# A new order of the whole instruction list, other engines for some copies and block sums, and 130 zero matmuls instead of 82

## The chip, the cores and the metric

The kernel runs on one core of a Trainium2 chip. The metric is the device time of one launch in microseconds (us), inputs in HBM at the start and the output in HBM at the end. Four compute engines work side by side, each on its own queue strictly in order: PE (matrix multiply, with its weight loads in the row PEld), DVE (vector), ACT (activation) and POOL (general purpose). SP only issues DMAs. An instruction that needs what another engine makes waits at the head of its queue, and everything behind it in that queue waits too.

## The reference

Cross attention in both directions between 512 tokens and 32 states for 8 batches and 8 heads, followed by a two layer network with a leaky activation.

```python
# x (8, 8, 512, 64), state (8, 8, 32, 64)
scores = scale * x @ state^T ; a  = softmax(scores)  ; xread = a  @ state
scores2 = scale * state @ x^T; a2 = softmax(scores2) ; sread = a2 @ x
attn = concatenate([xread, sread], axis=2)           # (8, 8, 544, 64)
x = attn.transpose(0, 2, 1, 3).reshape(8 * 544, 512)
h = x @ w_in                                          # w_in (512, 2048)
g = maximum(h, 0) + alpha * minimum(h, 0)
out = g @ w_out                                       # w_out (2048, 512), out (4352, 512)
```

## The kernel before

All tensors are held in 16 bit floats on chip; matmuls accumulate in 32 bit. The 512 tokens of a batch never pass through `xread`: since `xread @ w_in = a @ (state @ w_in)`, the kernel multiplies the states with `w_in` (step `m`, copied out of PSUM by `mo`) and then the softmax weights with that product (step `F`, or `f` for half a contraction, `h` in the profile). There are 16 column blocks of `h` for each of the batches 0 to 7. Each goes through two elementwise steps: `N` (ACT writes relu(-h), "neg") and `G` (DVE makes g from neg, 1 - alpha and h, into the tile "gp"). "Batch 8" is a ninth set of rows: the 256 state rows of all batches (`sread`), collected by `rd` and `rdo`, with its own `F.8`, `N.8`, `G.8` of half the width.

The second layer is done in two ways. Batch 0 uses plain matmuls (`S`, 2 of 128x512 each, copied out by `O`). Batches 1 to 8 use a seven product block scheme: `P.b.p.c` is a quarter of product p of batch b (4 matmuls of 128x256; 2 for batch 8), the sums and differences of blocks of g are made by `A.b.i.grp` ("s"), those of `w_out` by `T.i.part` ("ws"), and `Q` copies or adds the products out. The last output block of batch 7 is done by plain matmuls in three pieces (`M`, `MO`).

The softmax of the tokens' weights for batch b runs through four engines: `sc` (PE, scores), `sb` (DVE, 32x32 transposes), `smax` (DVE), `ssh` (POOL, subtract the maximum), `sexp` (ACT), `ssum` (DVE), `snorm` (POOL), `wb` (DVE, transposed back to "aT"). `F.b` needs `wb.b`. The other direction goes `tm` or `tx`, `ty` (maximum), `te` (ACT, exp), `tsum`, `tn` (normalise), `tt` (transposing DMA), `rd`. Batch 0 does the first chain in two halves, its steps having a third number 0 or 1.

Input loads that change the type are issued by POOL in its queue: `lx0`, `lx.b` (x), `lst` (states), `wi.f` and `wo.i` (quarters of the weights, 512 KB each as they land). x of batches 0 and 1 is transposed by PE (`xt`, copied by `xo`), of the others by a transposing DMA on SP's queue (`xd`). Half of x of batch 0 and the states of batch 0 come in by SP's and ACT's DMAs in 32 bits and are cast on chip (`xc`, `stc`); `stt` and `sto` are the transposition of batch 0's states and its copy, `str` and `sro` the same for all other states; `id` makes the identity matrix that the transposes need; `oma` makes 1 - alpha. `Z.k.n` issues n matmuls of zeros into PSUM bank k, whose result nobody reads.

The order of all of this is written out in the list `ORDER`, one word for each step; the loop at the end of the kernel issues the steps in that order, and each engine receives its own steps in the order of the list. In a word the numbers are the step's arguments; a last number is a PSUM bank (k0 to k5 are single banks; steps without one use a shared pair of banks called "two"), a last letter is the engine: a is ACT, v is DVE, p is POOL, and d (for `A`) an accumulating DMA issued by POOL. A bank is taken again only when the last reader of its former tile is done.

The list decides four things: the order on each queue, the bank of each PSUM tile, the engine of each copy and block sum, and how many zero matmuls stand where.

Of the kernel before, what the change touches and what calls it, by code (L numbers as in the profile page):

```python
# [29 lines left out]
smax.1 N.0.11 S.0.2.3 m.0.3 G.0.8 F.0.10.5 tn.0.1 T.0.0.p T.0.1.p S.0.0.3 mo.0.3.a.0 G.0.9 N.0.10  # L30
G.0.11 ssh.p.1 T.2.0.p S.0.3.0.3 mo.0.3.v.1 S.0.3.1 F.0.13.0 S.0.3.2 sexp.1 N.0.13 G.0.10 S.0.3.3
m.1.3 ssum.1 G.0.13 F.0.14.5 S.0.2.4 snorm.p.1 T.1.0.p N.0.14 G.0.14 S.0.1.4 wb.1 tt.0 F.0.12.0
N.0.12 G.0.12 S.0.0.4 F.0.15.5 S.0.3.4 mo.1.3.a.1 N.0.15 tsum.1 tn.1.0 S.0.1.5 G.0.15 S.0.0.5
# [2 lines left out]
F.1.0.2 O.0.0.a T.3.0.p G.1.3 S.0.1.7 N.1.0 S.0.3.5 smax.2 te.2.1 F.1.5.4 S.0.3.6 O.0.1.a G.1.0
F.1.1.5 N.1.5 ssh.p.2 S.0.3.7 G.1.9 N.1.1 F.1.2.1 O.0.3.a G.1.1 F.1.6.2 N.1.2 F.1.4.0 W.O.0.3 G.1.5
T.2.1.p F.1.8.3 sexp.2 W.O.0.2 P.1.1.0.5 G.1.2 N.1.4 rd.0.4 ssum.2 N.1.6 rd.1.1 rdo.0.a lx.4 P.1.1.1
rdo.1.a xd.3 F.1.11.4 G.1.4 N.1.8 snorm.p.2 F.1.12.1 te.2.0 G.1.6 F.1.10.0 N.1.11 G.1.8 m.2.3 N.1.10
F.1.15.2 G.1.11 F.1.13.3 N.1.12 A.1.3.0.p P.1.1.2 G.1.10 mo.2.3.a.1 W.O.0.1 P.1.2.0.4 mo.2.3.a.0  # L40
# [792 lines left out]
```

## Time and profile before

| | |
|---|---|
| median of 3 runs | 210.06 us (209.83 to 210.15) |
| span of the profiled execution | 208.5 us |
| median less that span (start and end of the launch that the span leaves out) | 1.6 us |
| PE busy in the span | 200.2 us, 96% |
| DVE, POOL, ACT busy | 175.2, 180.9, 145.5 us |

The profile covers one execution. The profiled execution's own launch time is not given apart from its span; the span and the 1.6 us around it make the median. The lines of the profile name the engine, the line of the kernel, the operation, what it writes and reads, and durations in us; "x16" is a count. Durations of matmuls include the time until the result lies in PSUM, so that those of neighbouring matmuls overlap: the spacing of starts, not the duration, is what a matmul costs in a stream. The step names used here are not in the profile; a step is found there by its line number (`N` is L551, `G` L569, `F` L519 and for batch 8 L528, `P` L668, `S` L588, `m` L486, `mo` L508, `Z` L245, `A` L645 and by DMA L621, `T` L616, `tn` L440 on ACT and L442 otherwise) and by its place in the list.

### The profile page before, as it was taken

What the parts mean: (1) busy time and instruction counts of PE and PEld (TensorE: products, weight loads), DVE (VectorE), ACT (ScalarE), POOL (GpSimd) and SP (SyncE); (2) the same over time, 40 slices, a digit from 0 to 9 for tenths busy, and PEclk for the clock granted to TensorE, in tenths of its full rate; (3) what the DMA queues carried; (4) which work ended last, traced back from release to release, by engine and by line L of the source; (5) the groups of instructions that cost most, each with busy time, mean ns of one, the idle gap of its engine ahead of it and who ended that gap; (6) DMA issues with size and microseconds to landing.
All of it is one profiled execution on the core that took longest, in us unless ns stands there. A gap on an engine that the chain in (4) does not pass through costs nothing.

```text
span 208.5 us, 5136 instructions
## 1 busy us (share of the span) xinstructions
PE 200.2 (96%) x2034; PEld 135.3 (65%) x2034; DVE 175.2 (84%) x273; ACT 145.5 (70%) x291; POOL 180.9 (87%) x119
## 2 busy tenths in 40 slices
PE   7789999999999999999999999999999999999993
PEld 6554344346557775766677776666678777888882
DVE  1697998999999999999999999998995987744431
ACT  4298996699998899988889579778654545451110
POOL 7579948999999999999999999979996972969960
PEclk9999999999999999999999999999999999999999
DMA  6999999599979949999997166035401144234143
GB/s 148 177 204 208 205 203 149 103 132 191 218 144 142 116 58 212 206 126 165 183 225 100 43 146 166 24 82 151 104 0 53 23 78 154 37 63 156 50 153 104
DMA packets 44793, 27.11 MB, mean 130 GB/s; under 512 B 22097, under 2 KB 42465, under 8 KB 44769
## 3 DMA queue, kind: packets, MB, share of 16 engines
q0 software_dynamic: 14192, 12.03, 38.5%
q1 hardware_dynamic: 29872, 14.23, 31.1%
q10 hardware_dynamic: 704, 0.52, 0.8%
q8 instruction: 16, 0.26, 0.5%
q14 instruction: 9, 0.07, 0.1%
HBM read 17.31 MB, written 8.91 MB: 126 GB/s over the span
## 4 chain that ended last, share of the span: by engine, by line
PE 70%; DVE 14%; ACT 5%; DMA 4%; POOL 3%; issue 2%; DVEq 0%; POOLq 0%
PE p L668 41%; PE h L519 18%; DVE gp L569 8%; DMA w_in_sb<-in_moe_w_in_dram 4%; PE h L528 3%; PE m_ps L486 3%; PE sr_ps L461 2%; ACT m L508 1%; DVE aT L397 1%; ACT neg L551 1%; DVE m L508 1%; POOL s L645 1%; ACT e L424 1%; POOL an L387 1%; PE o L588 1%
## 5 line engine op out<-in xcount | busy, mean ns | idle before, releaser
L551 ACT ACTIVATE neg<-h 128x512 f32<-128x512 f32 (+1 forms) x144 | 78.5, 583 | 27.4 <-PE h L519 18.5
L569 DVE SCALAR_TENSOR_TENSOR gp<-neg,oma_sb,h 128x512 f16<-128x512 f32 x128 | 89.0, 735 | 6.7 <-ACT neg L551 6.4
L519 PE MATMUL h<-aT,m 128*128 128x512 f16 x250 | 68.6, 379 | 0.3 <-DVE gp L569 0.3
L645 POOL TENSOR_TENSOR s<-gp,s 128x1024 f16<-128x1024 f16 x28 | 65.7, 2393 | 1.2 <-DVE gp L569 0.6
L668 PEld LDWEIGHTS <-gp 128*128 128x128 f16 x432 | 41.7, 98 | 13.9 <-issue 1.9
L668 PEld LDWEIGHTS <-s 128*128 128x128 f16 x368 | 35.2, 98 | 12.7 <-POOL s L645 1.7
L668 PE MATMUL p<-ws,s 128*128 128x256 f16 x248 | 37.3, 273 | 0.2 <-POOL s L645 0.2
L645 POOL TENSOR_TENSOR s<-gp 128x1024 f16<-128x1024 f16 x14 | 31.6, 2260 | 6.5 <-DVE gp L569 6.4
L519 PEld LDWEIGHTS <-m 128*128 128x128 f16 x250 | 23.6, 98 | 16.1 <-issue 3.3
L668 PE MATMUL p<-ws,gp 128*128 128x256 f16 x224 | 33.6, 273 | 0.0
L508 ACT CAST m<-m_ps 128x512 f16<-128x512 f32 x51 | 28.8, 600 | 4.8 <-PE m_ps L486 3.6
L668 PE MATMUL p<-w_out_sb,gp 128*128 128x256 f16 x208 | 30.6, 273 | 0.0
L371 POOL TENSOR_TENSOR ts<-ts,mx 128x1024 f32<-128x1024 f32 (+1 forms) x9 | 17.1, 1905 | 6.0 <-DVE mx L365 6.0
L668 PE MATMUL p<-w_out_sb,s 128*128 128x256 f16 x120 | 18.3, 273 | 0.0
L387 POOL TENSOR_TENSOR an<-ts,r 128x1024 f16<-128x1024 f32 (+1 forms) x9 | 16.3, 1808 | 1.8 <-DVE r L382 1.8
L588 PE MATMUL o<-w_out_sb,gp 128*128 128x512 f16 x64 | 16.6, 380 | 0.1
L621 POOL DMA_DIRECT2D gp<-gp x14 | 13.2, 962 | 3.4 <-issue 2.9
L569 DVE SCALAR_TENSOR_TENSOR gs<-neg,oma_sb,h 128x256 f16<-128x256 f32 x16 | 7.2, 478 | 8.2 <-ACT neg L551 8.2
L486 PE MATMUL m_ps<-w_in_sb,stT 64*32 64x512 f16 x256 | 11.7, 383 | 0.3 <-DMA w_in_sb<-in_moe_w_in_dram 0.2
L588 PEld LDWEIGHTS <-gp 128*128 128x128 f16 x64 | 5.9, 98 | 8.1 <-issue 1.3
L424 ACT ACTIVATE e<-sc,nb 128x512 f16<-128x512 f32 x16 | 11.0, 693 | 0.1
L699 ACT COPY p<-p 128x512 f32<-128x512 f32 x11 | 6.5, 588 | 6.4 <-PE p L668 6.4
(76 smaller groups left out, 248.9 us busy)
## 6 DMA issues: line engine op xcount, KB each, us to landing
out_dram<-c SPq DMA_DIRECT2D x27, 256.0 KB, 3.1
xg<-in_x_dram POOLq DMA_DIRECT2D x7, 512.0 KB, 8.7
gp<-gp POOLq DMA_DIRECT2D x14, 256.0 KB, 3.6
w_in_sb<-in_moe_w_in_dram POOLq DMA_DIRECT2D x4, 512.0 KB, 11.8
w_out_sb<-in_moe_w_out_dram POOLq DMA_DIRECT2D x4, 512.0 KB, 13.1
...
```

Of the source, the lines that this page charges most:

```text
L371: engine(e).tensor_tensor(ts, ts, over_blocks(cols(live["mx", b], j, S // N)), ALU.subtract)
L387: engine(e).tensor_tensor(blocks(cols(live["an", b], j, S)), blocks(cols(live["ts", b], j, S)), over_blocks(cols(live["r1", b], j, S // N) ...
L424: nc.scalar.activation(live["e2", b][:, g, :, :], live["sc", b][:, :, :, g, :].rearrange("p r j s -> p (r j) s"), EXP, bias=live["nb", b][ ...
L486: nc.tensor.matmul(t[N * k : N * (k + 1), :], st_head(b, h)[64 * r : 64 * r + 64, :], w_in_sb[64 * r : 64 * r + 64, c, 512 * f : 512 * (f ...
L508: copier(e)(m_tile(b)[:, f, g, :], live["mp", b, f][g])
L519: nc.tensor.matmul(h.rearrange("p (r j s) -> p r j s", r=2, j=2), ms[b][:, f, g, 128 * j : 128 * (j + 1)], weights(b, g), start=(g == 0), ...
L551: nc.scalar.activation(neg, h, RELU, bias=0.0, scale=-1.0)
L569: nc.vector.scalar_tensor_tensor(gt, negs.pop((b, jc)), oma_sb[:, jc : jc + 1], h, ALU.mult, ALU.add)
L588: nc.tensor.matmul(outs[b, q], token_cols(b, jc, q), w_out_sb[:, jc, :], start=(jc == 0), stop=(jc == n_jc - 1),)
L621: nc.gpsimd.dma_start(gp[:, 1, 0], gp[:, 1, 1], accum_op=ALU.add)
L645: engine(e).tensor_tensor(t, x, y, op)
L668: nc.tensor.matmul(chains[chain][:, t, :], lhs, rhs[:, i, :], start=(opens and i == 0 and t == 0), stop=(i == half_k - 1), skip_group_chec ...
```

## The change

The list `ORDER` is replaced from its first word to its last. In the new list

- there are 8 groups of zero matmuls (20, 16, 12, 18, 9, 24, 21, 10) instead of 10 (20, 9, 7, 6, 4, 3, 5, 12, 7, 9), all of them before the first `f` or `F` of batch 0 as before;
- 14 of the 50 block sums `A` made by POOL are given to DVE (10 of full size, 4 of batch 8), and 1 of the 8 `T`; the 14 made by a DMA stay;
- `tn`: POOL 2 instead of 6, ACT 9 instead of 10, DVE 5 instead of 0;
- copies `mo`: DVE 4 instead of 13, ACT 60 instead of 51; `Q`: DVE 27 instead of 31, ACT 28 instead of 24; `xo`: DVE 6, ACT 2 instead of 7 and 1; `rdo`: DVE 2, ACT 6 instead of 3 and 5; `sro`: one on DVE instead of both on ACT; `xc` has its two engines exchanged; `stc` is on ACT, for which the step takes an engine as an argument;
- all PSUM banks are given out anew.

The numbers of all other instructions and DMAs are the same. Only the parts of the two lists that are spoken of are shown.

```diff
 ORDER = """
-lx0 id lst stc xc.1.v xc.0.a oma wi.0 lx.1 Z.1.20 stt.0 Z.2.9 xt.0.1.0.1 xt.0.0.0.2 xo.0.1.0.v
-xo.0.0.0.v sto.a Z.0.7 sc.0.0 Z.0.6 xt.0.1.1.3 xt.0.0.1.4 str.0.5 sb.0.0 xo.0.0.1.v xo.0.1.1.a Z.1.4
-sc.0.1 smax.0.0 str.1.0 sro.0.a wi.1 sb.0.1 wo.0 smax.0.1 wi.2 ssh.p.0.0 sro.1.a sexp.0.0 Z.1.3 sc.0
-m.0.0.1.2 ssh.p.0.1 mo.0.0.a.0 Z.5.5 m.1.0.3.4 m.2.0.5.0 tm.0 mo.2.0.a.0 ssum.0.0 sexp.0.1
-mo.1.0.a.0 mo.2.0.a.1 wo.1 Z.1.12 m.3.0.1.5 Z.3.7 xt.1.1.0.3 snorm.p.0.0 mo.1.0.v.1 te.0.1
-mo.3.0.a.1 ssum.0.1 wb.0.0 xt.1.0.0.4 xo.1.1.0.v te.0.0 xo.1.0.0.v wi.3 xt.1.1.1.0 snorm.p.0.1 Z.3.9
-f.0.0.0.5 mo.0.0.a.1 xo.1.1.1.v xt.1.0.1.3 wo.2 f.0.2.0.4 tsum.0 m.1.1 wb.0.1 mo.3.0.a.0 xo.1.0.1.v
-m.0.1.0.2 mo.1.1.v.0 tn.0.0 mo.0.1.v.0 f.0.2.1 f.0.0.1 mo.1.1.a.1 mo.0.1.a.1 f.0.1.0.1 f.0.1.1
-F.0.3.3 m.4.0 N.0.0 N.0.1 F.0.5.2 N.0.2 F.0.4.0 G.0.0 G.0.1 N.0.3 G.0.2 F.0.7.5 N.0.5 N.0.4 G.0.3
-S.0.1.0.1 mo.4.0.a.0 S.0.0.0.4 mo.4.0.a.1 G.0.4 S.0.0.1 S.0.1.1 lx.2 N.0.7 m.0.2.3.0 sc.1 G.0.5
-mo.0.2.a.0 S.0.2.0.2 wo.3 G.0.7 m.1.2.5.3 mo.0.2.a.1 mo.1.2.a.0 S.0.2.1 sb.1 F.0.6.0 xd.2 mo.1.2.a.1
...
-S.0.2.5 mo.1.3.a.0 m.2.1 tn.1.1.a F.1.7.0 mo.2.1.v.0 S.0.2.6 N.1.7 mo.2.1.v.1 F.1.3.5 lx.3 tt.1
-G.1.7 sc.2 S.0.2.7 tx.2 T.1.1.p F.1.9.0 O.0.2.a S.0.0.6 N.1.3 S.0.1.6 sb.2 N.1.9 S.0.0.7 ty.2
...
-P.8.3.2 W.MO.7.1 P.8.4.1 P.8.3.3 P.8.4.2 Q.8.c12.v M.7.2.3 P.8.4.3 MO.7.2.v W.Q.8.c12 Q.8.c21.a
-WA.MO.7.2 W.Q.8.c21
+xc.0.v stc.a lx0 lst wi.0 oma id Z.1.20 stt.0 sto.a lx.1 xc.1.a Z.1.16 xt.0.0.0.0 xt.0.1.0.1 xo.0.0.0.a wi.1
+xo.0.1.0.v Z.2.12 sc.0.0 sb.0.0 smax.0.0 ssh.p.0.0 Z.2.18 xt.0.1.1.1 wo.0 wi.2 xt.0.0.1.0 xo.0.1.1.a
+xo.0.0.1.v Z.2.9 sc.0.1 sb.0.1 sexp.0.0 str.0.0 sro.0.v smax.0.1 str.1.1 sro.1.a Z.2.24 m.1.0.1.0 m.2.0.2.3
+ssum.0.0 mo.1.0.a.0 wo.1 mo.2.0.a.0 mo.1.0.v.1 wi.3 sc.0 m.3.0.4.5 tm.0 mo.3.0.a.1 Z.1.21 xt.1.0.1.5 ssh.p.0.1
+sexp.0.1 m.0.0.0.2 ssum.0.1 xt.1.1.0.1 mo.3.0.a.0 te.0.0 mo.2.0.a.1 xo.1.1.0.v lx.2 te.0.1 snorm.p.0.0
+xt.1.0.0.4 wb.0.0 xt.1.1.1.1 mo.0.0.a.0 mo.0.0.a.1 Z.3.10 m.1.1 mo.1.1.a.1 m.0.1.0.3 f.0.0.0.2 xo.1.0.1.v
+xo.1.1.1.v mo.1.1.a.0 snorm.p.0.1 wb.0.1 f.0.0.1 N.0.0 mo.0.1.v.0 mo.0.1.v.1 xo.1.0.0.v wo.2 f.0.1.0.1 f.0.1.1
+N.0.1 T.0.0.p f.0.2.0.0 f.0.2.1 G.0.0 N.0.2 G.0.1 F.0.3.5 N.0.3 F.0.7.3 G.0.3 G.0.2 m.4.0 F.0.4.2 F.0.5.4
+mo.4.0.a.0 N.0.4 wo.3 G.0.4 lx.3 N.0.7 G.0.7 S.0.1.0.1 mo.4.0.a.1 T.0.1.p S.0.0.0.5 S.0.0.1 N.0.5 G.0.5 sc.1
+tm.1 m.0.2.2.0 mo.0.2.a.1 S.0.1.1 sb.1 F.0.6.3 mo.0.2.a.0 m.1.2.0.4 tsum.0 tn.0.0.p mo.1.2.a.1 N.0.6 G.0.6
+F.0.11.2 mo.1.2.a.0 N.0.11 te.1.0 S.0.0.2 smax.1 ssh.p.1 G.0.11 S.0.2.0.4 S.0.2.1 S.0.2.2 te.1.1 S.0.1.2
+F.0.9.0 tsum.1 S.0.0.3 N.0.9 G.0.9 tn.0.1.v m.0.3 mo.0.3.a.0 mo.0.3.a.1 S.0.2.3 F.0.8.3 N.0.8 S.0.1.3 F.0.10.2
+G.0.8 N.0.10 T.1.0.p F.0.13.0 N.0.13 sexp.1 tn.1.0.v m.1.3 G.0.10 G.0.13 mo.1.3.a.1 S.0.3.0.3 xd.2 S.0.3.1
+mo.1.3.a.0 S.0.3.2 S.0.3.3 ssum.1 snorm.p.1 F.0.14.0 T.1.1.p N.0.14 F.0.12.2 N.0.12 tn.1.1.a G.0.14 m.2.1
+mo.2.1.a.1 S.0.3.4 S.0.0.4 T.2.0.v F.0.15.0 N.0.15 T.2.1.p S.0.2.4 G.0.12 S.0.0.5 T.3.0.p S.0.0.6 mo.2.1.a.0
+sc.2 S.0.2.5 tt.1 S.0.2.6 G.0.15 S.0.2.7 O.0.2.a wb.1 F.1.9.0 S.0.0.7 sb.2 N.1.9 tt.0 xd.3 O.0.0.a F.1.7.4
...
+M.7.0.3 P.7.3.3 W.Q.8.c12 Q.7.c22.v P.7.4.0 P.7.4.1 P.7.4.2 MO.7.0.v P.7.4.3 Q.7.c12.v W.Q.7.c22 Q.7.c21.v
+W.MO.7.0 P.8.4.0 P.8.4.1 W.Q.7.c12 P.8.4.2 P.8.4.3 Q.8.c21.v M.7.2.0.2 M.7.2.1 M.7.2.2 M.7.2.3 MO.7.2.v
+M.7.1.0.3 M.7.1.1 M.7.1.2 M.7.1.3 W.Q.7.c21 MO.7.1.v W.Q.8.c21 W.MO.7.1 WA.MO.7.2
 """
...
-    def first_states_cast():
+    def first_states_cast(e):
         live["st0"] = consts.tile([128, 2, D], F16, name="st0")
-        nc.vector.tensor_copy(live["st0"], st0_32)
+        copier(e)(live["st0"], st0_32)
```

More of the change, by code (lines that the diff above doesn't have):

```diff
@@ L30 @@
[L30 to L33, printed above, removed]
-S.0.2.5 mo.1.3.a.0 m.2.1 tn.1.1.a F.1.7.0 mo.2.1.v.0 S.0.2.6 N.1.7 mo.2.1.v.1 F.1.3.5 lx.3 tt.1
-G.1.7 sc.2 S.0.2.7 tx.2 T.1.1.p F.1.9.0 O.0.2.a S.0.0.6 N.1.3 S.0.1.6 sb.2 N.1.9 S.0.0.7 ty.2
@@ L36 @@
[L36 to L40, printed above, removed]
@@ new lines @@
+W.Q.1.c22 F.2.15.0 tsum.4 tn.3.0.a ssum.3 N.2.15 G.2.15 P.1.4.0 P.1.4.1 P.1.4.2 P.1.4.3 m.3.1 A.2.3.1.v
+mo.3.1.a.0 P.2.1.0.5 P.2.1.1 F.2.14.1 P.2.1.2 A.2.3.0.p P.2.1.3 tn.3.1.a tt.3 mo.3.1.a.1 Q.1.c21.a A.2.2.0.p
+N.2.14 rd.2.2 rdo.2.a G.2.14 xd.5 Q.2.p1.a m.4.3 P.2.2.0.0 P.2.2.1 mo.4.3.a.0 P.2.2.2 P.2.2.3 Q.1.c12.v
+m.5.1.3.1 mo.4.3.a.1 mo.5.1.a.1 mo.5.1.a.0 snorm.p.3 wb.3 m.4.2 W.Q.1.c21 P.2.6.0 A.2.2.1.p Q.2.c11.v smax.4
+F.3.3.2 N.3.3 G.3.3 F.3.2.0 N.3.2 G.3.2 F.3.7.3 N.3.7 G.3.7 mo.4.2.a.0 F.3.10.1 N.3.10 G.3.10 P.2.6.1 F.3.8.2
```

136 lines of the change are left out of this document (63 added, 73 removed).

## The prediction

> **What bounds the kernel now.** I read the page's busy line first, then busy time by stretches, the chain of work that ended last, and PE's waits; after that the first 38 us in order of time.
>
> ```profile
> span 208.5 us, 5136 instructions
> ...
> PE 200.2 (96%) x2034; PEld 135.3 (65%) x2034; DVE 175.2 (84%) x273; ACT 145.5 (70%) x291; POOL 180.9 (87%) x119
> ```
> ```profile
> 0.00:20.00 20.00, 16.08 (x243) 10.91 (x244) 13.15 (x32) 12.14 (x22) 14.84 (x22) 1.00 1.10 183
> 20.00:38.00 18.00, 17.55 (x118) 6.91 (x116) 16.88 (x25) 15.07 (x30) 14.54 (x9) 1.00 1.26 190
> 38.00:140.00 102.00, 101.71 (x1070) 66.41 (x1070) 99.82 (x142) 88.38 (x179) 99.57 (x59) 1.00 0.80 139
> 140.00:205.00 65.00, 64.83 (x608) 51.06 (x605) 45.34 (x77) 29.56 (x62) 52.00 (x32) 1.00 0.32 85
> ```
>
> The columns of the stretches are PE, PEld, DVE, ACT and POOL, then PE's clock. From 38 to 205 us PE has records over 166.5 of 167 us. DVE and POOL are nearly as full until 140 us (99.8 and 99.6 of 102). Whether PE's time is dense is told by the spacing in the chain and by what PE's waits are called:
>
> ```profile
> 64.20 1.75 PE p L668 x16
> ...
> 80.75 2.16 PE h L519 x10
> ```
> ```profile
> PEld L486 <- issue: 4.7, 15, 0.4
> ...
> PEld L668 <- POOL s L645: 1.7, 5, 0.5
> ```
>
> 1.75/16 is 0.109 us for a product matmul, 2.16/10 is 0.216 us for an `F` matmul. With each kind of step at its cheapest spacing in this trace, the list's matmuls other than zeros add up to 185.2 us; of the time from 38 us on, only 5.0 us are left over, nearly all of it about 0.1 us apiece where 64x32 tiles (`m`, `sc`, `rd`) and 128x128 tiles follow each other, which the first wait above shows as "issue". The longest wait for POOL is 0.5 us. So **PE's own work is the bound behind 38 us**, and no order can win more than about 1 us there. What an order can win is at the start, where PE's records cover 33.6 of 38 us with zero matmuls among them, and at the end.
>
> **The start, step by step.** The walk below uses these rows.
>
> ```profile
> 1.10 2.31 PE L245 MATMUL z<-zero 128*128 128x128 f16 x20 [1.10 <-DVE zero L239]
> ...
> 2.52 0.29 POOL masks.py:199 TENSOR_SCALAR_AFFINE_SELECT ident<-ident 128x128 f16<-128x128 f16 x1
> ...
> 3.35 0.78 POOL L226 DMA_DIRECT2D w_in_sb<-in_moe_w_in_dram  x1
> ...
> 3.48 0.43 PE L260 MATMUL st_ps<-ident,st 128*64 128x128 f16 x4
> ...
> 6.45 0.80 POOL L226 DMA_DIRECT2D w_in_sb<-in_moe_w_in_dram  x1
> ...
> 6.95 0.30 PE L326 MATMUL sc<-xT,stT 64*32 64x256 f16 x8 [0.72 <-DVE xT L317]
> ...
> 9.62 2.22 ACT L294 COPY stT<-st_ps 128x896 f16<-128x896 f16 x2 [0.70 <-PE st_ps L260]
> 9.66 1.05 POOL L371 TENSOR_TENSOR ts<-ts,mx 128x512 f32<-128x512 f32 x1 [2.41 <-DVE mx L365]
> ...
> 11.57 0.41 PE L486 MATMUL m_ps<-w_in_sb,stT 64*32 64x512 f16 x8 [0.18 <-DMA w_in_sb<-in_moe_w_in_dram]
> ...
> 12.86 0.84 PE L245 MATMUL z<-zero 128*128 128x128 f16 x12
> ...
> 13.97 1.06 ACT L508 CAST m<-m_ps 128x512 f16<-128x512 f32 x2
> ...
> 18.89 0.59 PE L519 MATMUL h<-aT,m 128*128 128x512 f16 x2
> ...
> 19.62 3.07 ACT L551 ACTIVATE neg<-h 128x512 f32<-128x512 f32 x6
> ...
> 20.27 4.70 DVE L569 SCALAR_TENSOR_TENSOR gp<-neg,oma_sb,h 128x512 f16<-128x512 f32 x7 [1.05 <-ACT neg L551]
> ...
> 21.73 2.14 PE L588 MATMUL o<-w_out_sb,gp 128*128 128x512 f16 x8
> ...
> 32.29 3.17 SPq L304 DMA_TRANSPOSE xT<-xg  x1
> ...
> 36.05 1.25 DVE L397 STREAM_TRANSPOSE aT<-an 128x1024 f16<-128x1024 f16 x1 [0.44 <-POOL an L387]
> ...
> 38.36 0.61 PE L519 MATMUL h<-aT,m 128*128 128x512 f16 x2
> ```
> ```profile
> DMA to landing us min/median/max: 8.2/11.8/15.4
> ```
> ```profile
> L424 ACT ACTIVATE e<-sc,nb 128x512 f16<-128x512 f32 x16 | 11.0, 693 | 0.1
> ```
>
> *To 12 us.* `lst` and the first `wi` go ahead of `id` on POOL, so the identity is ready at about 4.2 us instead of 2.8, and `stt` starts at 4.2 instead of 3.48; `xc.1`, behind `sto` on ACT, ends at 5.8. `sc.0.0` still starts at about 6.95, since its two copies `xo` are now split between ACT and DVE. Then `smax` stands directly behind `sb`, and `ssh` starts at 8.8 instead of 9.66. The 48 more zeros cost 0.055 us each (0.84 us for twelve, less the last one's latency), 2.7 us, all while PE waits for data: `Z.2.24` ends at 12.04, and `m.1.0` behind it needs the second state copy, whose half of the 2.22 us ends at 11.95. So the first `m` starts 0.5 us later than 11.57.
>
> *The loads.* The first `wi`, issued at 3.35, lands 8.2 us later, at 11.5; the fourth load behind it, issued at 6.45, has the longest landing, 15.4 us, at 21.85. So loads of 512 KB land 2.6 us apart from a queue that is never empty, and `wo.0` and `wi.2` behind a POOL subtraction cost nothing: issued at 9.9 and 10.6, they are some 5 us ahead of their turn. But four issues of 0.78 now stand ahead of `ssh.0.1`, and `lx.2` ahead of `snorm.0.0`: these start at 12.9 and 14.9.
>
> *12 to 22 us.* ACT has twelve steps between 12.5 (the first `m` done) and its first `N`: ten at 0.53 (1.06 for two) and two `te` at 0.69, so `N` comes at 19.2 instead of 19.62 and the first `G` at 19.8 instead of 20.27. PE's `f` wait for `mo.0.0` until 18.2; six at 0.216 put the first `F` at 19.5, later than 18.89. Then `F.0.7`, `m.4.0`, `F.0.4` (whose bank the first `G` frees at 20.5) and `F.0.5` follow, and the first `S` comes at 21.45, with the same steps done as before at 21.73: **0.3 us ahead**.
>
> *22 to 38 us.* Walked the same way with `G` every 0.66 us (4.70 for seven), `F.0.11` ends at 25.4, where before is at `S.0.2.1`: two `F` done against one `S`, 0.4 ahead. Before opens batch 1 at 38.36 with nine `S` steps and `sc.2` left to do; the new list opens it with eight `S` left and `sc.2` done, 0.43 + 0.34 = 0.77 us further. But `wb.1` must be done. Its `snorm` now stands behind `T.1.0` on POOL, which waits for `wo.2`, and that lands one load later than before since `lx.2` is ahead of it, beside the transposing DMA `xd.2`, now issued when `lx.2` lands, near 29.5 instead of 32.29. I put 1.0 us on that meeting; batch 1 then opens at 38.8 instead of 38.36, and **0.3 us remain**.
>
> **The rest: prices of the moved work.**
>
> ```profile
> L508 DVE CAST m<-m_ps 128x512 f16<-128x512 f32 x13 | 8.7, 679 | 0.0
> ...
> L706 DVE TENSOR_TENSOR c<-p,p 128x512 f32<-128x512 f32 x13 | 8.9, 684 | 1.1 <-PE p L668 0.7
> ...
> L645 POOL TENSOR_TENSOR s<-gp,s 128x1024 f16<-128x1024 f16 x28 | 65.7, 2393 | 1.2 <-DVE gp L569 0.6 <-PE p L668 0.2
> ...
> L442 POOL TENSOR_SCALAR e<-e,r 128x512 f16<-128x512 f16 x6 | 9.7, 1665 | 0.1
> ```
>
> POOL loses ten full `A` and one `T` (11 x 2.35), four half `A` (4 x 1.2) and four `tn` (4 x 1.67): 37 us. DVE loses nine `mo` and four `Q` (13 x 0.68, 9 us). What it gains, an operation on two 16-bit tensors in SBUF, has no row. The 1.25 us of `wb`, also 1024 elements, is the upper bound; the lower is half of that, nothing excluding two elements a step. I take 1.25, nearest in shape: 11 x 1.25 + 4 x 0.62 + 5 `tn` x 0.65 = 19.5, so DVE's total rises by some 10 us, mostly behind 130 us, where it idles (45.3 of 65 us busy). Adding up DVE's list against PE's from the first `F.1` on, the `G` that PE needs next came up to 0.95 us late by such sums in the old list; in the new one it is 0.4 to 2.3 us early at this price and at least 1.6 at the lower one. ACT's 13 more `mo` and `Q` (7 us) lie on 13.6 idle us between 38 and 140 and on 35 behind. None of it reaches PE: cost 0, and the cover is that margin.
>
> **The end.**
>
> ```profile
> 204.51 0.38 PE L668 MATMUL p<-ws,gs 128*128 128x256 f16 x2
> 204.72 0.28 DVE L728 TENSOR_TENSOR osb<-p,o 128x128 f32<-128x128 f32 x1
> 204.83 1.20 SPq L579 DMA_DIRECT2D out_dram<-c  x2
> 204.93 0.37 ACT L703 COPY c<-p 128x256 f32<-128x256 f32 x1 [4.24 <-PE p L668]
> ```
>
> Behind the last matmul stand a 0.37 us copy, the second of two issues of 0.6, and a 128 KB store. The new list ends on a 64 KB piece by an addition of 0.28. I take 0.4 us off.
>
> **Sum.** 208.5 - 0.3 - 0.4 = 207.8 in the span, with the 1.6 us around it 209.4; against the median of 210.06 that is 0.3% less. A measurement of this kernel can tell about 0.2% (0.42 us) from no change.
>
> **Rivals.** *DVE's new sums and POOL block each other (slower).* Twenty steps (15 sums, 5 `tn`) join DVE's queue beside a POOL still busy some 70% of the time. If such a step waits for the POOL operation under way, it loses up to 2.4 us, on average 0.7 x 1.2 = 0.8; ten stand ahead of 140 us, each with the `G` behind it: 8 us of delay against a margin of 0.4 to 2.3 that every stall of PE restores. I price it at 2.2 us on PE, 211.6. From 0.15 us a step on it eats the forecast's 0.7 past the bound. For it: `T.2.0` stands ahead of `G.0.12`, which `S.0.0.6` needs soon. Against: POOL's lighter list lets several of them meet an idle POOL, and no row shows such a pair, since DVE's additions in this trace have an operand in PSUM. The Trainium skill (SBUF — State Buffer, section "Who interferes with whom") says that a DVE instruction with two SBUF inputs contends with a GpSimd instruction that reads SBUF, and that the later one fully blocks. By that rule the sum is this rival's 211.6, without it 209.4; nothing in this trace decides.
>
> *PE's fast clock comes later (slower).* The first 20 zeros took 0.10 us each (2.31 us), later ones 0.055, though the clock column reads 1.00 throughout: the array starts at half speed. The new list leaves PE idle from 3.2 to 4.2 us, before the change of speed. If that delays it, the 36 zeros and transposes ahead of `sc.0.0` take 1.6 us more, of which waits for data hide part: about 1.0 reaches `m`, `N` and `S`, 210.4. The Trainium skill (TensorE: Matmul & The Clock Gate, section "What's actually happening") has the clock released after a busy window of about 3.4 us, which a gap may spoil.
>
> *Nothing is gained (same).* The 0.3 us is a difference of sums over some forty steps; if `wo.2` or `xd.2` comes 0.7 us later than put here, 210.1.
>
> **Chances.** Forecast: 0.46, own range 208.5 to 209.6. DVE against POOL: 0.31. Clock: 0.11, of it 0.05 within the bound. Nothing gained: 0.12, of it 0.05 slower. So faster 0.46, same 0.12, slower 0.42. The range reaches from 208.4 (0.8 at the start, 0.6 at the end, 0.3 of tile switches) to 212.4 (the first rival with 3 us on PE).
>
> **What would show it.** Right: first `S` near 21.4 us, first `F.1` near 38.8 with `sc.2` done, PE covering 166.5 of 167 us behind it, the last store issued within 0.4 us of the last matmul. Wrong: `F` waiting for "gp" by over 1 us in all, a DVE `s` row well over 1.25 us, zeros at 0.10 us behind 4.5 us, or `an` held up by the `T` that waits for "w_out_sb".

## The result, and the profile after

The changed kernel takes 224.77 us (median; 223.42 to 226.45), the kernel before 209.94 us beside it: a ratio of 1.071, with a 95% interval of 1.065 to 1.077. Here and below, medians and ratios leave out slow executions, those over 1.5% above the fastest of the same kernel; one of the changed kernel's four, of 228.94 us, is such a one. The changed kernel is slower by 14.8 us where 0.7 us less was forecast, and lies beyond the range of 208.4 to 212.4. The profiled execution took 226.45 us, with a span of 224.7.

The page's first lines of the changed kernel, and below them its busy time by stretches, with the columns as in the prediction:

```profile
span 224.7 us, 5224 instructions
...
PE 206.2 (92%) x2082; PEld 140.1 (62%) x2082; DVE 195.1 (87%) x278; ACT 150.5 (67%) x305; POOL 148.3 (66%) x100
```
```profile
0.00:20.00 20.00, 17.26 (x278) 14.31 (x279) 12.66 (x29) 11.61 (x22) 14.47 (x22) 1.00 1.11 183
20.00:38.00 18.00, 16.29 (x126) 6.26 (x125) 17.91 (x26) 15.25 (x32) 10.70 (x8) 1.00 1.31 197
38.00:140.00 102.00, 94.82 (x981) 59.38 (x980) 96.36 (x122) 82.63 (x171) 83.73 (x48) 0.98 0.77 124
140.00:205.00 65.00, 61.50 (x545) 45.54 (x545) 57.78 (x90) 38.62 (x79) 35.45 (x23) 1.00 0.31 73
```

PE's own work is the 185.2 us of the prediction in both kernels, since only zeros were added. So the span holds 39.5 us beside that work (224.7 - 185.2) and held 23.3 before: 16.2 more. From 38 to 140 us PE has records over 94.8 of 102 us, before over 101.7. That is where the time went, with some more on either side. POOL is emptier and DVE fuller, as the change intended: DVE's total rose by 19.9 us where the prediction had some 10.

PE's waits name two kinds of lateness. The columns are total us, times, longest us:

```profile
PE h L509 <- DVE gp L559: 7.6, 5, 3.0
...
PE sc L316 <- DMA xT<-xg: 2.0, 1, 2.0
PE o L578 <- DVE gp L559: 1.2, 1, 1.2
...
PE st_ps L250 <- POOL ident masks.py:199: 1.0, 1, 1.0
PE p L658 <- DVE s L635: 1.0, 2, 0.5
```

In the kernel before, the first of these waits was

```profile
PE h L519 <- DVE gp L569: 0.3, 1, 0.3
```

*The held sums.* 9.8 us are waits for DVE (7.6, 1.2 and 1.0). The groups of the new DVE steps show why: they take 1.4 to 2.1 us in the mean, where the prediction took 1.25 for a sum and 0.65 for a `tn`.

```profile
L635 DVE TENSOR_TENSOR s<-gp,s 128x1024 f16<-128x1024 f16 x8 | 11.3, 1414 | 0.1
...
L432 DVE TENSOR_SCALAR e<-e,r 128x512 f16<-128x512 f16 x5 | 8.4, 1677 | 0.0
...
L606 DVE TENSOR_TENSOR ws<-w_out_sb 128x1024 f16<-128x1024 f16 x1 | 2.1, 2122 | 0.0
```

The timeline around 105 us shows one of them in order of time (start, length, engine):

```profile
104.87 1.82 POOL L611 DMA_DIRECT2D gp<-gp  x2 [3.32 <-DVE gp L559]
...
105.53 3.87 DVE L635 TENSOR_TENSOR s<-gp,s 128x1024 f16<-128x1024 f16 x1
...
106.09 2.75 POOL L635 TENSOR_TENSOR s<-gp,s 128x1024 f16<-128x1024 f16 x1
```

`A.3.2.1` sits on DVE from 105.53 to 109.40, behind POOL's `A.3.2.0`, which ends at 108.84. Six of the eleven full sums of this trace take 0.68 or 0.69 us, with at most 0.13 us of that beside a POOL operation that computes; a held one ends 0.55 us behind the POOL operation. `A.3.2.1` began 0.56 us ahead of `A.3.2.0`, while POOL was issuing the two `A.3.1`, and was held all the same. Behind it in DVE's queue are the `G` for which PE then waits 2.95 us:

```profile
102.42 0.59 PE L509 MATMUL h<-aT,m 128*128 128x512 f16 x2 [0.35 <-DVE gp L559]
110.11 0.89 PE L509 MATMUL h<-aT,m 128*128 128x512 f16 x2 [2.95 <-DVE gp L559]
117.77 0.41 PE L316 MATMUL sc<-xT,stT 64*32 64x256 f16 x16 [2.00 <-DMA xT<-xg]
```

*The clock.* That idle stretch had a second price. By stretches, the seventh column is PE's clock:

```profile
108.00:110.20 2.20, 0.09 (x1) 0.09 (x1) 2.20 (x3) 0.27 (x1) 0.84 (x1) 1.00 1.44 184
110.30:113.60 3.30, 3.30 (x12) 1.50 (x11) 2.46 (x4) 0.60 (x2) 1.68 (x1) 0.50 1.60 59
113.70:117.00 3.30, 2.07 (x24) 1.40 (x22) 1.91 (x3) 2.54 (x5) 3.30 (x3) 1.00 0.96 139
```

After 3 us without a matmul the clock reads 0.50 for 3.41 us, and the eleven matmuls in it, five of `F` and six of `P`, cost 1.7 us more. The Trainium skill (TensorE: Matmul & The Clock Gate, section "What's actually happening") has the array go to half rate after an idle window of about 3.4 us. The half rate lasts one such length here, but the idle stretch ahead of it is only 2.95 us. The length of a wait alone does not decide it: waits of 2.94 us in `c2` and 2.84 us in `d1`, two of the runs below, brought no half rate, and waits of 2.19 us in `c2` and 1.48 us in `d2` did.

*The pile of transfers.* The third row above waits for `xd.6`, the transposing load of x. DMAs issued at 103.2 and at 104.9 to 105.5 in the changed kernel, then `xd.6` of the kernel before, issued at 93.46 (the last column is us from issue to landing):

```profile
gp<-gp POOLq DMA_DIRECT2D x2, 256.0 KB, 11.7
xT<-xg SPq DMA_TRANSPOSE x1, 14.5
```
```profile
xT<-xg SPq DMA_TRANSPOSE x1, 4.7
```

In the new list `lx.6` is issued at 94.90 instead of 84.75, so `xd.6` goes out 10 us later, 1.7 us ahead of the two accumulating DMAs `A.3.1`. At its issue `lx.7` (98.46 to 107.54) and the transposing DMA `tt.5` (101.86 to 108.60) are still in flight, and a store and `xd.7` follow before it has landed.

### The profile page after: what moved, and what is told of

The parts are those of the page before. It is cut to its first block, busy times and chain, and to the rows that moved or that the text cites. A ratio compares the mean times of both kernels' runs of the same rounds, so it can differ in the third digit from the quotient of the medians.

```text
span 224.7 us, 5224 instructions
## 1 busy us (share of the span) xinstructions
PE 206.2 (92%) x2082; PEld 140.1 (62%) x2082; DVE 195.1 (87%) x278; ACT 150.5 (67%) x305; POOL 148.3 (66%) x100
## 5 line engine op out<-in xcount | busy, mean ns | idle before, releaser
L635 POOL TENSOR_TENSOR s<-gp,s 128x1024 f16<-128x1024 f16 x20 | 45.8, 2376 | 3.5 <-DVE gp L559 3.3
L498 ACT CAST m<-m_ps 128x512 f16<-128x512 f32 x60 | 34.0, 597 | 4.9 <-PE m_ps L476 4.8
L635 POOL TENSOR_TENSOR s<-gp 128x1024 f16<-128x1024 f16 x12 | 26.0, 2173 | 12.0 <-DVE gp L559 11.8
L658 PE MATMUL p<-ws,s 128*128 128x256 f16 x248 | 33.5, 274 | 0.5 <-DVE s L635 0.5
L658 PE MATMUL p<-ws,gp 128*128 128x256 f16 x224 | 29.2, 273 | 0.3 <-DMA gp<-gp 0.3
L658 PE MATMUL p<-w_out_sb,gp 128*128 128x256 f16 x208 | 28.0, 276 | 0.3 <-DVE gp L559 0.3
L361 POOL TENSOR_TENSOR ts<-ts,mx 128x1024 f32<-128x1024 f32 (+1 forms) x9 | 15.9, 1763 | 10.6 <-DVE mx L355 8.8
L658 PE MATMUL p<-w_out_sb,s 128*128 128x256 f16 x120 | 16.4, 273 | 0.5 <-DVE s L635 0.5
L399 DVE TENSOR_REDUCE nb<-sc 128x2 f32<-128x1024 f32 x8 | 9.7, 1215 | 3.2 <-PE sc L316 3.0
L476 PE MATMUL m_ps<-w_in_sb,stT 64*32 64x512 f16 x256 | 12.1, 384 | 0.1
L689 ACT COPY p<-p 128x512 f32<-128x512 f32 x13 | 7.8, 598 | 5.9 <-PE p L658 5.8
L235 PE MATMUL z<-zero 128*128 128x128 f16 x130 | 10.7, 248 | 1.1 <-DVE zero L229 1.1
## 6 DMA issues: line engine op xcount, KB each, us to landing
w_in_sb<-in_moe_w_in_dram POOLq DMA_DIRECT2D x4, 512.0 KB, 10.6
```

The lines of the kernel that those rows point to most:

```text
L235: nc.tensor.matmul(t, zero, zero, start=True, stop=True)
L361: engine(e).tensor_tensor(ts, ts, over_blocks(cols(live["mx", b], j, S // N)), ALU.subtract)
L476: nc.tensor.matmul(t[N * k : N * (k + 1), :], st_head(b, h)[64 * r : 64 * r + 64, :], w_in_sb[64 * r : 64 * r + 64, c, 512 * f : 512 * (f ...
L498: copier(e)(m_tile(b)[:, f, g, :], live["mp", b, f][g])
L635: engine(e).tensor_tensor(t, x, y, op)
L658: nc.tensor.matmul(chains[chain][:, t, :], lhs, rhs[:, i, :], start=(opens and i == 0 and t == 0), stop=(i == half_k - 1), skip_group_chec ...
```

## The experiments

### What u1_pairs shows: which DVE steps POOL holds up

> The kernel leaves the whole computation out and writes a constant; it only runs four of each of seven DVE operations, first alone, then beside a chain of POOL additions (128x1024, 16 bit), then three of them beside POOL multiplications and beside POOL subtractions in 32 bit. Lock theory: the sum of two 16 bit tensors takes 0.69 us alone and about 2 to 2.8 us beside POOL, each one ending some 0.5 us behind the end of a POOL operation; the multiplication of a 16 bit tile (the form of tn) takes 0.3 to 0.4 us alone and is held in the same way. The addition with an operand in PSUM, the step G's form, the 32x32 transposition and the maximum take the same alone and beside POOL. Rival (POOL merely slows the memory that both share): every form becomes longer by a like share, no form by a factor of 3.

The first fence has the means of four steps each alone, the second of four each beside POOL's chain of 128x1024 subtractions.

```profile
L71 DVE STREAM_TRANSPOSE dc<-da 128x1024 f16<-128x1024 f16 x4 | 5.0, 1243 | 0.1
...
L61 DVE TENSOR_TENSOR dc<-da,db 128x1024 f16<-128x1024 f16 x4 | 2.8, 690 | 0.1
L67 DVE TENSOR_TENSOR osb<-neg,h 128x512 f32<-128x512 f32 x4 | 2.7, 685 | 0.1
L65 DVE COPY dc<-da 128x1024 f16<-128x1024 f16 x4 | 1.7, 425 | 0.1
L63 DVE TENSOR_SCALAR e<-e,r 128x512 f16<-128x512 f16 x4 | 1.4, 352 | 0.1
```
```profile
L61 DVE TENSOR_TENSOR dc<-da,db 128x1024 f16<-128x1024 f16 x4 | 10.0, 2511 | 3.4 <-POOL da L96 3.3
L63 DVE TENSOR_SCALAR e<-e,r 128x512 f16<-128x512 f16 x4 | 8.7, 2168 | 0.1
L65 DVE COPY dc<-da 128x1024 f16<-128x1024 f16 x4 | 7.1, 1768 | 0.1
L71 DVE STREAM_TRANSPOSE dc<-da 128x1024 f16<-128x1024 f16 x4 | 5.0, 1243 | 0.1
...
L67 DVE TENSOR_TENSOR osb<-neg,h 128x512 f32<-128x512 f32 x4 | 2.7, 684 | 0.1
```

The sum goes from 0.69 to 2.51 us, the form of `tn` from 0.35 to 2.17, a 16 bit copy from 0.43 to 2.22 where it is held (the first of the four fell into a gap). The transposition and the addition with an operand in PSUM do not change at all, nor do the maximum and `G`'s form. So this is no sharing of a memory: some forms are shut out, the others not touched. POOL pays as well: its subtractions grow from 2.12 to 2.44 us where a sum was let in between. The Trainium skill (SBUF — State Buffer, section "Who interferes with whom") says nearly this: a DVE step with two SBUF inputs contends with a GpSimd step that reads SBUF, a DVE step in a mode that uses two ports (copies and multiplications by a column among them) contends with GpSimd as well, and whoever issues first shuts the other out for its whole instruction. The rows beside subtractions agree that the two engines exclude each other.

What POOL is doing matters, though. Beside its multiplications by a column (1.56 to 1.82 us each) a sum took 0.90 us in the mean and 1.17 at most, so there it is hardly held, and that rule of the Trainium skill is too strong; beside 32 bit subtractions it took 2.74.

```profile
L61 DVE TENSOR_TENSOR dc<-da,db 128x1024 f16<-128x1024 f16 x4 | 3.6, 902 | 11.1 <-POOL da L96 11.0
```

### u3_forms: a form of the sum that is not held

> The kernel leaves the whole computation out; it runs six DVE forms three times each, alone and then beside a chain of POOL additions: the sum of two 16 bit tensors, the same as a three operand step (product with a column, then difference), a multiplication as a three operand step, a sum written in 32 bit, a sum of 32 bit tensors and a copy from 32 to 16 bit. Theory (only the forms that run at more than one element a cycle are held): the plain 16 bit sum, 0.69 us alone, takes 2.5 beside POOL; the forms that take about 1.1 us alone for 1024 elements take the same beside POOL. Rival (every step with two operands in SBUF is held): all but the copy end 0.5 us behind a POOL operation, at 2 us or more.

The three operand form, alone and beside POOL, then the copy from 32 to 16 bit beside POOL:

```profile
L64 DVE SCALAR_TENSOR_TENSOR dc<-da,r,db 128x1024 f16<-128x1024 f16 x3 | 3.9, 1285 | 0.1
```
```profile
L64 DVE SCALAR_TENSOR_TENSOR dc<-da,r,db 128x1024 f16<-128x1024 f16 x3 | 9.1, 3019 | 0.1
...
L72 DVE CAST dc<-ts 128x1024 f16<-128x1024 f32 x3 | 7.5, 2486 | 0.1
```

The theory (only forms of more than one element a cycle) falls. All six forms are held, those of 1.2 to 1.3 us too, and the copy from 32 bit as well, which the rival left out. None of the four ways of writing a sum of two SBUF tensors that ran here (plain, three operands, 32 bit result, 32 bit inputs) escapes POOL's subtractions; what is left is where it stands.

### Giving the work back: a1_pool_sums and a2_early_back

`a1` gives the fifteen sums back to POOL and the five `tn` to ACT; `a2` does it for the ten steps ahead of 160 us. Nothing else is changed.

```diff
-... tn.0.1.v ... tn.1.0.v ... T.2.0.v ... A.2.3.1.v ... A.3.2.1.v ...
+... tn.0.1.a ... tn.1.0.a ... T.2.0.p ... A.2.3.1.p ... A.3.2.1.p ...
```

> The new list with the fifteen sums that it gives to DVE given back to POOL and its five DVE normalisations given to ACT; order, banks and zeros stay. Theory L (DVE and POOL lock each other out): the stalls behind the twenty steps go, 11 to 13 us in the new list's trace with the half clock that one of them brought on; POOL carries some 31 us more. Expected 211 to 214 us, no F row waiting for gp by more than 0.6 us. Rival O (the new order itself stalls, above all by the loads and transposes that meet at 103 to 118 us): 219 us or more.

> The same, but for the ten of the twenty that stand before 160 us alone (five normalisations to ACT, T.2.0 and four sums to POOL); the ten late sums stay on DVE. Theory L with PE as the bound: late sums meet a DVE with idle time, and only about 0.7 us of stalls behind 160 us is theirs, so this is within 1.5 us of the run with all twenty back. If late sums cost as much as early ones, it lies half-way, near 218 us.

Measured: 231.48 us for `a1` (ratio 1.102, 1.094 to 1.109), 6.7 above the changed kernel. The four executions of `a2` spread from 225.51 to 233.12 and give no verdict. Without the holds POOL itself is late: PE waits for POOL's sums for 7.4 us in the trace of `a1` and for 4.3 in that of `a2`. In both the step `P.2.6.0`, for which the order wants `A.2.2.0`, starts 1.0 us late and `F.3.3` behind it another 2.5. My theory gave 211 to 214. What fell is the belief that a list built around sums on DVE can have them on POOL at the same places; the hold itself was not tested by these two, and a wait for `xd.6` stood in both (1.8 and 0.5 us).

### b1_dve_sums and h1_old_no_hold: the hold in the old order

`b1` is the kernel before with the same fifteen sums and five `tn` on DVE. `h1` keeps that, but each such step is a 32x32 transposition of half the tile, which takes the same time and is not held:

```diff
-        engine(e).tensor_tensor(t, x, y, op)
+        if e == "v":
+            src = x if i in (1, 3) else y
+            nc.vector.transpose(t[:, :, :128], src[:, :, :128])
...
```

> The old list with the same fifteen sums and five normalisations given to DVE, nothing else. Theory L: DVE steps of up to 3 us, each as long as the POOL operation that it meets, and 5 to 15 us more than 209.9. Rival O: DVE's total rises by about 10 us, mostly where it idles, POOL's falls by about 35 us, and the time stays within 1.5 us of 209.9.

> b1_dve_sums (the kernel before with fifteen sums and five multiplications on DVE) with each of these replaced in its place by a 32x32 transposition of half the tile, as in c1_no_lock: the same queue, nearly the same time on DVE (0.65 us for 0.69), but a form that POOL does not hold up. The sums and multiplications are left out of the computation. If the hold is the price: 209.5 to 211.5 us, 7 to 9 us less than b1_dve_sums. If the work on DVE or POOL's changed times are the price: 215 us or more.

Measured: `b1` 218.93 us (1.043, 1.041 to 1.045), within the theory's 5 to 15 us more, and `h1` 212.78 (1.013, 1.010 to 1.015). One row of each, a sum in `b1` and its stand-in in `h1`:

```profile
L645 DVE TENSOR_TENSOR s<-gp,s 128x1024 f16<-128x1024 f16 x8 | 9.3, 1174 | 0.1
```
```profile
L658 DVE STREAM_TRANSPOSE s<-s 128x512 f16<-128x512 f16 x10 | 6.8, 690 | 0.0
```

Of the 9.0 us that `b1` loses, 6.2 are the hold. The other 2.8 are more than I had put for the work itself (up to 1.5); no row of `h1` names one wait for them, and they stay unexplained.

### c1_no_lock, c2_id_first, c3_both: one cause at a time in the new order

`c1` is the changed kernel with the stand-ins of `h1`; `c2` makes the identity ahead of the state load, as before; `c3` does both.

```diff
-xc.0.v stc.a lx0 lst wi.0 oma id Z.1.20
+xc.0.v stc.a lx0 id lst wi.0 oma Z.1.20
```

> The changed kernel with the 15 block sums and 5 multiplications on DVE each replaced, in the same place of the same queue, by a 32x32 transposition of half the tile (512 elements, some 0.65 us; 256 elements for tn). These sums and multiplications are left out of the computation. POOL's work, PE's work, the order and the banks are those of the changed kernel. Lock theory: the stalls behind the DVE sums vanish, 11 to 13 us of the 16, so 212.5 to 214.5 us, with no idle stretch of PE over 2 us and no half clock behind 10 us. Rival (the new order makes POOL, DVE or the transfers late whatever the sums do): 219 us or more, with the stalls near 107, 115 and 139 us still there.

> The changed kernel with the identity made ahead of the state load, as in the kernel before. Clock theory: PE's idle microsecond ahead of the first transposition is gone, the full clock comes near 4.5 us and not at 7.9, sc.0.0 starts near 7.0, the first S at 21.5 to 22.0 and the time falls by 0.8 to 1.3 us, to 224.3 to 224.8. Rival (the stalls behind take the gain back): the first S comes earlier but the time stays within 0.5 us of the changed kernel's.

> The edits of the two kernels ahead of this in one (the same sums and multiplications are left out). If both causes are real and independent the gains add up: 11 to 13 us and 0.8 to 1.3 us less than the changed kernel, 211.2 to 213.8 us. If the sums alone carry the loss: 212.5 to 214.5. If the new order itself is bad: 218 us or more.

Measured: 224.90, 225.71 and 224.64 us, all within 1.0 us of the changed kernel. With the holds gone nothing was won, though the stalls behind them are gone from the traces of `c1` and `c3`. Taken alone that would speak against the hold, but the trace of `c3` shows what took its place; PE's waits for transposing loads, the longest of them, and the landing of `xd.6`:

```profile
PE sc L316 <- DMA xT<-xg: 13.8, 2, 11.0
```
```profile
121.17 0.63 PE L316 MATMUL sc<-xT,stT 64*32 64x256 f16 x16 [10.99 <-DMA xT<-xg]
```
```profile
xT<-xg SPq DMA_TRANSPOSE x1, 19.0
```

The shorter of the two, 2.8 us, stands at `sc.2` for `xd.2`, at 40.8 us; behind 45 us a single wait of 11 us stands at `sc.6`, and every other is below 0.5 us. PE came there at 110.2 instead of 115.8, and `xd.6`, issued at 102.1, landed at 121.1. With the 4.7 us that it takes in the kernel before it would have been there at 106.8, so the slow landing is to blame and not the later issue. Both waits bring the half clock with them, and the matmuls in it cost some 4.4 us more (half of the 8.7 us of matmul time in these stretches). This execution took 228.09 us, 3.4 above the median of `c3`, so its waits are longer than usual. In the changed kernel the holds had run down much of the same time before PE got to the load. `c2` shows the same on a small scale: the first `S` came at 21.50 instead of 22.79 (the full clock at 6.16, where 4.5 was expected), and the time did not fall.

### d1, d2, d3: the transfers apart

`d1` is `c2` with five words moved, so that `lx.3` comes later, `lx.6` and `lx.7` earlier, `xd.6` directly behind them and `xd.7` ahead of `tt.5`. `d2` is the same with the stand-ins of `c1`. `d3` differs from `d2` in the place of `lx.6` alone.

```diff
-... wo.3 G.0.4 lx.3 ... te.5.1 lx.6 ... N.3.12 xd.6 ... Q.2.c21.a lx.7 ... sc.6 xd.7 ...
+... T.1.1.p lx.3 ... snorm.p.3 lx.6 ... A.2.4.1.p lx.7 xd.6 ... W.Q.2.c11 xd.7 ...
...
-snorm.p.3 lx.6 wb.3 ... A.2.1.1.d G.3.1
+snorm.p.3 wb.3 ... A.2.1.1.d lx.6 G.3.1
```

> The changed kernel with the identity ahead of the state load and with DMA words moved so that transposing loads of x meet neither accumulating DMAs nor a row of large loads: lx.3 goes behind T.1.1, lx.6 and lx.7 go earlier (behind snorm.3 and A.2.4.1), xd.6 directly behind lx.7 and xd.7 ahead of tt.5. The computation is whole and the DVE sums stay. Two causes in turn (theory): the transposing load xd.6 lands within 6 us instead of 14.5, sc.6 no longer waits, but the DVE sums held by POOL still cost their 8 to 12 us behind it, so 219 to 223 us. Rival (the meeting of the DMAs is all of it): 212 us or less. Rival (DMAs do not matter): within 1.5 us of the 225.8 us of the run with the identity first.

> The edits of the kernel ahead of this and the transpositions in place of the DVE sums and multiplications (these are left out of the computation). Two causes in turn: with both taken away PE finds nothing late any more, 209.5 to 213 us, with no wait over 1 us behind 45 us; each taken away alone left the time at 219 or more. If a third cause (POOL or DVE late by the order itself) carries several us: 215 us or more, and the waits of PE name it.

> d2_dma_apart_no_lock with one word moved: lx.6 goes from behind snorm.3 to behind A.2.1.1, so that it no longer meets xd.5 and the two A.2.1 (the sums on DVE are left out of the computation, as there). If the 3 us that d2 has above the kernel before are that meeting: P.2.5 near 86 us finds its sums, and the time is 209.3 to 210.8. If they are the new order itself: 212 us or more.

| | transfers as in the change | transfers apart |
|---|---|---|
| sums held | 225.71 (`c2`) | 223.62 (`d1`; ratio 1.062, 1.055 to 1.069) |
| sums not held | 224.64 (`c3`) | 213.00 (`d2`; 1.012, 1.008 to 1.016) |

This square settles it. With the transfers apart, the hold costs 10.6 us (223.62 - 213.00). With the holds gone, the meeting of the transfers costs 11.6 (224.64 - 213.00). Each alone accounts for most of the loss, and together they cost 12.7, not 22.3: PE waits through the same time once. In `d1` `xd.6` lands 7.4 us after its issue, where 6 was expected, and the time is 0.6 us above the range given. `d2` keeps one wait of 1.5 us for an accumulating DMA, at 88.5 us, with the half clock behind it; `d3` is free of both and brings 2.5 us more, to 210.45 (1.0025, 1.0005 to 1.0045). The waits of PE in `d1`, then its stretch from 38 to 140 us in `d3`:

```profile
PE h L509 <- DVE gp L559: 7.4, 5, 2.8
PE o L578 <- DVE gp L559: 1.5, 2, 1.2
...
PE p L658 <- DVE s L635: 1.0, 2, 0.5
```
```profile
38.00:140.00 102.00, 100.20 (x1048) 65.34 (x1047) 96.64 (x135) 88.70 (x183) 88.90 (x53) 1.00 0.82 135
```

The wait for the load is gone from `d1`, and the waits for held sums are all still there, 9.9 us. Without both, and with five DMA words moved, the new order stands 0.5 us (0.1 to 0.9) above the kernel before. So it has no gain of its own that these two would have hidden.

### e1_xd6_meets_A: the meeting in the old order

> The kernel before with one word moved: lx.6 goes behind lx.7, so that the transposing load xd.6 is issued some 4 us later, at about 97.5 us, just when the two accumulating DMAs A.3.1 are issued (97.99 and 98.61). The computation is whole. Theory (a transposing and an accumulating DMA bring each other nearly to a stop): xd.6 and both A.3.1 land 8 to 20 us after issue instead of 3.4 to 4.7, sc.6 near 105.6 waits for xd.6, and the time rises by 3 to 13 us. Rival (the DMAs share the engines fairly): xd.6 lands by 104 and the time stays within 0.5 us of 209.9.

```diff
-N.3.5 lx.6 rd.3.3 ... P.2.7.3 lx.7 mo.4.1.a.0
+N.3.5 rd.3.3 ... P.2.7.3 lx.7 lx.6 mo.4.1.a.0
```

Measured: 213.12 us (1.013, 1.007 to 1.020), 2.8 us more for one word. In the profiled execution, at 211.71 us the shortest of its runs, `xd.6` takes 7.0 us instead of 4.7, and PE waits for it:

```profile
xT<-xg SPq DMA_TRANSPOSE x1, 7.0
```
```profile
106.19 0.41 PE L326 MATMUL sc<-xT,stT 64*32 64x256 f16 x16 [1.52 <-DMA xT<-xg]
```

The direction is that of the theory, the sizes are below it: a landing time of 8 to 20 us and 3 to 13 us of time were expected, and the two `A.3.1` landed after 3.7 and 5.5 us. The meeting here has fewer parts than that of the changed kernel; whether it is milder for that was not tested.

### u2_dma_pairs and u4_dma_turns: the transfers by themselves

> The kernel leaves the whole computation out; it issues the transposing load of x (T), one or two accumulating additions of 256 KB (A), a store (S), a load of x (L) and a second transposing load (U), first alone, then together, each group waiting for the one before. Theory: T alone lands in about 4.3 us, A alone in 3.3, two A in 4.3; T and two A together take 8 us or more, and with a store and a second transposing load 12 to 20; T with a store, or two A with a store, stay within the sum of the two. Rival (the engines share fairly): no group takes longer than the sum of its parts alone.

> The kernel leaves the whole computation out; groups of one or two transposing loads (T, U) and two accumulating additions (AA), in both orders, some with a pause of 1.25 us between the first and the second kind, each group waiting for the one before. Fair sharing: T alone 4.3, AA 4.3, TU 8.5, T and AA in any order at most 8.6 from first issue to last landing, TU and AA at most 13. If the order of issue matters (a transposing load that starts behind accumulating ones is held): AA before T takes 10 us or more, T before AA 7.5.

In `u2` a transposing load alone lands in 4.25 us, two accumulating DMAs in 4.30; issued together all have landed after 7.5, which is less than the sum. A store, two accumulating DMAs and a second transposing load, issued behind a first one, took 9 and 12 us for the last two in two groups, 12.1 and 14.8 us from the first issue to the last landing. From `u4`: a load issued 0.3 us ahead of two accumulating DMAs, one issued 1.0 us behind the first of them (each with the row of the DMAs beside it that were issued in the same stretch), and one issued 1.4 us ahead of the first:

```profile
gp<-gp POOLq DMA_DIRECT2D x2, 256.0 KB, 6.2
xT<-xg SPq DMA_TRANSPOSE x1, 7.5
```
```profile
gp<-gp POOLq DMA_DIRECT2D x1, 256.0 KB, 9.6
xT<-xg SPq DMA_TRANSPOSE x1, 9.3
```
```profile
xT<-xg SPq DMA_TRANSPOSE x1, 4.3
```

Behind accumulating DMAs the load takes 6.8 and 9.3 us, and 10.2 and 9.8 with a second load in the group; the load and the two accumulating DMAs of the second fence need 10.4 us in all, where the sum of the parts is 8.6. So both expectations hold in part: the transfers mostly share, and the order of issue adds up to 1.8 us. But the load that goes out 1.4 us ahead is not slowed at all, and `xd.6` of the changed kernel was 1.7 us ahead of `A.3.1`. So the meeting of these three does not by itself make its 14.5 us. The sum of what shares the time with it and is issued behind it comes near (4.25 for itself, 4.30, 4.25 for `xd.7` and 2.0 for the store, 14.8 us), but it leaves out `lx.7` and `tt.5`, which were in flight too, so the agreement shows nothing. Which transfer of the pile holds which, why `xd.6` took 11.1 us in `c2` but 19.0 in `c3`, and why the times of the kernels with the pile scatter by 5 to 7 us, stays open.

### a3_more_zeros and k1_id_late: the start

> The new list with the first group of zero matmuls made 32 instead of 20, which fills PE's gap between 3.2 and 4.4 us. Theory C (the gap put off the full clock from 4.5 to 7.9 us): the full clock comes near 4.5 us, sc.0.0 moves from 8.4 to about 7.0 us and the first S from 22.8 to about 21.5 us; in the whole, about 1 us less than the new list's 225.6, which may drown in that list's own scatter of 3 us. Without C: twelve more zeros cost nothing or up to 0.7 us, and the first S stays at 22.8 or later.

> The kernel before with one word moved: the identity is made behind the state load and the first quarter of w_in, as in the changed kernel. Clock theory: PE idles some 1 us ahead of stt.0, the full clock comes near 7.9 us and not at 4.5, sc.0.0 and with it the first m, N and S start 1.0 to 1.5 us later, and since PE has no slack behind, the whole time rises by 0.8 to 1.4 us, to 210.8 to 211.4. Rival (waits for loads hide it, or w_in coming earlier makes it up): within 0.3 us of the kernel before.

`a3` has 32 zeros in place of the first 20. The full clock came at 6.3 us instead of 7.9 (4.5 was expected) and the first `S` 0.7 us earlier, but the time is 224.71 (1.070, 1.067 to 1.074): within the changed kernel's. `k1` moves `id` behind `wi.0` in the old order. PE waits, and the full clock comes at 7.4 us instead of 4.5:

```profile
4.17 0.43 PE L260 MATMUL st_ps<-ident,st 128*64 128x128 f16 x4 [0.75 <-POOL ident masks.py:199]
```

Measured: 210.58 us, a ratio of 1.004 (1.002 to 1.007), so 0.9 us (0.3 to 1.4) for the late identity, at the low end of what the clock theory gave. That the clock is what costs it is not shown. In the profiled execution of `k1` the first `S` came 0.3 us before that of the kernel before, and executions of one and the same start differ by more. With the start of the kernel before, unchanged in `h1`, `b1` and `e1`, the full clock came at 4.52 (before), 5.08, 5.28 and 7.23 us, and the first `S` at 21.73, 22.09, 21.35 and 21.23: the latest clock has the earliest `S`.

### d4_mended: how much comes back with the whole computation

```diff
-... tn.7.0.v ... T.2.0.v ... A.3.3.1.p A.3.1.1.d ... G.4.14 A.3.2.1.v
+... tn.7.0.a ... T.2.0.p ... A.3.3.1.p A.3.2.1.v A.3.1.1.d ... G.4.14
```

> The changed kernel, with the whole computation, the identity first, the DMA words of d3_dma_spread, the five multiplications tn of DVE on ACT, T.2.0 back on POOL, and A.3.2.1 on DVE directly behind A.3.3.1, where POOL idles. Of the holds that cost PE something these are left: A.2.3.1 (0.5), A.4.4.1 (0.7), A.8.2.1 (0.6). If the two causes are all there is: 211 to 213.5 us. If moving the work to ACT and POOL makes them late, as it did with all sums in a1 and a2: 216 us or more.

Measured: 215.06 us (1.023, 1.020 to 1.027), 9.7 us better than the changed kernel, 1.6 above what I expected at most. Most of the sums that stay on DVE are not held:

```profile
L635 DVE TENSOR_TENSOR s<-gp,s 128x1024 f16<-128x1024 f16 x8 | 7.9, 992 | 0.2
```

`A.3.2.1` at its new place takes 0.69 us instead of 3.87. What is left are waits of 0.3 to 0.6 us behind the remaining holds and behind ACT, which now does the five `tn`. No version beat the kernel before.

## Why the prediction was wrong, point by point

*The step that failed: "None of it reaches PE: cost 0, and the cover is that margin".* It cost 10.6 us (`d1` against `d2`). The price was wrong on both sides. A sum that meets nothing takes 0.69 us, near the lower bound of 0.62; one that meets POOL takes 2.5 (`u1`) and up to 3.87. The 1.25 taken from `wb` was in neither case: `wb` is a transposition, a form that POOL does not touch. The margin of 0.4 to 2.3 us was worked out with the steps at prices that POOL does not enter; a single hold takes up to 3.2 us more than the sum itself (3.87 for 0.69). In the trace five waits for `h` and one for `S` are what came through.

*The first rival named the cause and mis-sized it.* "DVE's new sums and POOL block each other" was priced at 2.2 us on PE: ten steps at 0.8 us, less a margin "that every stall of PE restores". Measured, the waits for DVE are 9.8 us, and the half clock behind the longest one adds 1.7. The row on which I leaned against it ("no row shows such a pair") was true and no evidence: with no row on either side, the rule of the Trainium skill named there was the better guide. It held beside POOL's subtractions in `u1` and `u3`, though not beside the multiplications of `u1`.

*What was left out: the loads of the middle.* The walk followed `xd.2` but not `lx.6`, `lx.7`, `xd.6` and `xd.7`, which the new list issues next to `A.3.1`. Together with the meeting at `xd.2`, and without the holds, they would have cost 11.6 us (`c3` against `d2`). The loads of the middle were no rival and no term of the sum. For `xd.2` the meeting was seen ("beside the transposing DMA") and priced at 1.0 us; it was issued at 29.91, near the 29.5 given, and took 11.2 us instead of 6.0, for which PE waits 2.8 us in `c3`.

*The clock rival came true in part, and not in the sum.* The identity was ready late, the full clock came at 7.87 us instead of 4.52, and the first `S` at 22.79 instead of the 21.45 forecast. With the identity first, six traces of the new list (`c2`, `c3` and `d1` to `d4`) have the full clock at 6.1 to 7.2 us and the first `S` at 21.4 to 21.9. So the walk of the start was right within 0.5 us but for this. In the new order the whole time does not show it (`c2`), since the waits behind absorb it; in the old one the late identity costs 0.9 us (`k1`, forecast 1.0), whether by the clock or not. The Trainium skill (TensorE: Matmul & The Clock Gate, section "What's actually happening") lets the clock go up only after a busy window of about 3.4 us. The full clock is 3.35 us later here than in the kernel before, about one such window, but `e1`, which starts as the kernel before does, has it 2.71 us later, so that the gap of 1.0 us is the cause is not shown.

*The first `F.1` at 38.8* came at 43.27; with both causes gone it came at 39.5 (`d2`) and 40.3 (`d3`). So the walk was 0.7 to 1.5 us too early there, and the 0.3 us of gain was not to be had.

*The end* brought 0.2 us instead of 0.4: from the end of the last matmul to the end of the span it is 3.3 us, and was 3.6.

*That nothing is gained* was put at 0.12. With both causes taken away, the new order is 0.5 us slower than the old one (`d3`), so this rival describes the order itself; and "PE's own work is the bound behind 38 us" was a statement on the kernel before, which I carried over to the new list after adding up DVE's list alone, at prices without the hold.
